# Neighbouring query blocks share one window of keys: band matmuls in pairs in a block-sparse attention with a gated feed-forward

## The chip, the cores and the metric

The kernel runs on one core of one Trainium2 chip. The metric is the device time of one execution in microseconds (us), as the median of several runs; lower is better.

## What is computed

Block-sparse attention over `q`, `k`, `v` of shape (4, 8, 768, 64), then a gated feed-forward on its result. Cut to what matters:

```python
block, n_blocks, window, scale = 32, 24, 1, 1/8
mask = |blk_i - blk_j| <= 1                       # band: own block and both neighbours
mask |= (blk_i == 0) | (blk_j == 0) | (blk_i == 23) | (blk_j == 23)   # blocks 0 and 23 are global
for qb in range(24):                               # three sampled key blocks for each query block
    for kb in sampled_blocks[qb]: mask[qb, kb] = True
attn = softmax(where(mask, scale * q @ k.T, -1e9)); y = attn @ v      # per batch and head
x = y as (4, 768, 512)
h = relu(x @ w_in)                                 # 512 -> 1024
c = conv of h along the sequence, width 3, one weight per tap and feature
out = (h * sigmoid(c)) @ w_out                     # 1024 -> 512, float32
```

The sampled blocks are data: they are read on the chip, and entries that the band, the global blocks or an earlier entry already cover are pointed at a block of zeros.

## The kernel before

The work is cut into eight half batches n (batch b = n // 2, half g = n % 2, 384 queries each). A half batch has four attention steps, one for each pair of heads hp, and then a feed-forward. There are thus 32 attention steps. Each has four parts:

- **s_a, the band scores** (line 862): one matmul for each of the 11 inner query blocks, 128 keys on the output partitions, 64 columns (32 queries of two heads). Even and odd blocks use windows that begin at different 32-key offsets (`win`). **e_a** (line 871) takes the exponential on ScalarE, with a bias of -30000 on partitions (from `bias_t`) that are not of the block.
- **s_g, the global scores** (lines 882 and 887): six matmuls of the keys against the one fully attending block of this half ("full", block 0 or 23), and four of the two global key blocks (KD) against all inner queries. **e_g** (line 894) is their exponential.
- **s_r, the sampled scores** (line 905): 11 matmuls against gathered keys KG. **e_r** (line 912) is their exponential.
- **a_fn, attention times values** (line 951): the probabilities are the stationary operand, 32 query columns of them, and 65 value columns (64 and a one for the sum) stream through. The output of query block j lands on 32 of 128 PSUM partitions, 32j to 32j+31. For each step there are 67 matmuls: per inner block and head one band and one sampled, per inner block one global over both heads, and 12 for the full block. They are issued round robin over the four j.

The values come by way of a DRAM copy: `v` is loaded, cast and widened by the ones (line 674, `vr`), written to DRAM (`vs`, line 684, rows of 520 elements in sequence order), and read back as VN in six chunks of 128 rows (line 693). VS is VN shifted by 64 rows, a copy between partitions (line 702). The sampled values VG are gathered from `vs` by DMAs whose offset is a register (line 801), three for each block, 33 for each half batch; the sampled keys KG are copied inside SBUF with register offsets (line 791) by VectorE and GpSimd. `WHO` says which queue issues which gather: SyncE (SP) or GpSimd (POOL). The offsets are unpacked from a packed table by integer division, remainder and multiplication on the issuing engine (`block_off`, with loads of the table in `reg_load`, line 748); a limited number is kept in registers.

The feed-forward: line 1117 multiplies by w_in, lines 1128 and 1130 apply relu, lines 1031 to 1058 are the convolution and the gate on VectorE with a tanh on ScalarE (line 1046), a part of the convolution goes to TensorE (line 1078), and line 1001 multiplies by w_out.

The order of the instructions on all engines is fixed when the program is built: every piece of work is an operation with a cost for each engine that may do it, a due time and buffers (`pl.op`), and `Plan.run` searches for an order by forward and backward passes with random changes. Its costs are constants written in the code: a_fn counts as 0.74 us on TensorE, a change of the kind of matmul (`mode` "F", "T" or "A" of an operation) as SWITCH = 0.09 us, and fetching a page of 256 TensorE instructions as FETCH = 2.3 us. The plan knows no change of kind inside one operation.

At the start, QB (queries, with zeros for the other head) and other buffers are set to zero by VectorE and GpSimd (lines 519 to 535).

Of the kernel before, what the change touches and what calls it, by code (L numbers as in the profile page):

```python
# [52 lines left out]
class Op:  # L53
    __slots__ = ("alts", "fn", "prio", "deps", "lat", "dma", "mode", "allocs", "uses", "earliest", "outs",
                 "pend", "ready", "start", "end", "eng", "key", "done", "seq", "after", "lazy", "n", "nd")
# [9 lines left out]
DMA_LAT = 1.9  # L65
SWITCH = 0.09
LAZY = 12.0
PAGE, FETCH = 256, 2.3
# [3 lines left out]
class Plan:  # L72
# [11 lines left out]
    def op(self, alts, fn, prio, deps=(), lat=None, dma=None, mode=None, alloc=(), uses=(), earliest=0.0,  # L84
           after=(), lazy=False, n=0, nd=1):
        o = Op(alts, fn, prio, [d for d in deps if d is not None], lat, dma, mode, earliest)
        o.key = len(self.ops)
        o.lazy = lazy
        o.n = n
        o.nd = nd  # L90
        o.after = [d for d in after if d is not None]
        for b in alloc:
            o.allocs.append(b)
            b.users.append(o)
        for b in uses:
            o.uses.append(b)
            b.users.append(o)
        self.ops.append(o)
        return o
# [14 lines left out]
    def forward(self, prio, first=True):  # L114
# [8 lines left out]
        count, pages = 0, {}  # L123
# [13 lines left out]
        while left:  # L137
            still = []
            for o in blocked:
# [12 lines left out]
                if ok:  # L152
                    rr = {}
                    for e in o.alts:
                        t = r
                        for d in o.deps:
                            t = max(t, self.avail(d, e))
                        rr[e] = t
# [142 lines left out]
    def run(self, passes=6, trials=40):  # L301
# [9 lines left out]
        for x in range(trials):  # L311
            prio = [p + shake.gauss(0.0, 1.0) for p in best[1]]
# [12 lines left out]
def kernel(  # L325
# [21 lines left out]
    ROW = H * 65  # L347
    WHOLE = ()
    PEC = (2,)
# [11 lines left out]
    vs_t = [dr.tile([S + 32, ROW], BF16, tag=f"vs{x}", name=f"vs{x}") for x in range(B)]  # L361
# [4 lines left out]
    KT = many(NKT, [128, 4, S + 32], BF16, "kt")  # L366
# [10 lines left out]
    pa_t = many(NPA, [128, 704], BF16, "pa")  # L377
    pr_t = many(NPR, [128, 704], BF16, "pr")
    pg_t = many(NPG, [128, 736], BF16, "pg")
# [97 lines left out]
    def biases(e):  # L477
        nc.vector.memset(bias_t, 0.0)
        nc.vector.memset(bias_t[0:32], -30000.0)
        nc.vector.memset(bias_t[96:128, 1:2], -30000.0)  # L480
# [8 lines left out]
    def blocks(e):  # L489
# [16 lines left out]
        v_.tensor_scalar(out=tm, in0=r, scalar1=-1.0, scalar2=float(NB), op0=ALU.mult, op1=ALU.add)  # L506
# [11 lines left out]
    for s in range(NKT):  # L518
        z_ops.append(op({"POOL": 0.2}, lambda e, s=s: nc.gpsimd.memset(KT[s][:, :, S:S + 32], 0.0), -6))
    qz = []  # L520
    for s in range(NQB):
        def zq(e, s=s):
            eng = nc.vector if e == "DVE" else nc.gpsimd
            eng.memset(QB[s][0:64, 1, :], 0.0)
            eng.memset(QB[s][64:128, 0, :], 0.0)
        qz.append(op({"DVE": 0.8} if s < 4 else {"POOL": 1.7}, zq, -6 + s))
    kz = []
    for s in range(NKD):
        kz.append(op({"POOL": 0.25}, lambda e, s=s: nc.gpsimd.memset(KD[s], 0.0), -6 + s))
    vz = []  # L530
    for s in range(NVN):
        vz.append(op({"POOL": 0.6}, lambda e, s=s: nc.gpsimd.memset(VD[s].rearrange("p a b -> p (a b)"), 0.0), 1 + s))
# [14 lines left out]
    for b in range(B):  # L547
        vs_zero.append(sp(lambda e, b=b: nc.sync.dma_start(out=vs_t[b][S:S + 32, :], in_=zrow), 4 + 8 * b, [z_row],
# [40 lines left out]
    def qk_pair(P):  # L589
# [52 lines left out]
        def kd(e):  # L642
            kt = KT[kt_buf[b].index][:, hp, 0:S].rearrange("q (n s) -> q n s", s=32)
            for h in range(2):
                r0 = 64 * h
                nc.gpsimd.tensor_copy(out=KD[kd_buf[P].index][r0:r0 + 64, r0:r0 + 64]
                                      .rearrange("q (n s) -> q n s", s=32), in_=kt[r0:r0 + 64, 0:NB:NB - 1, :])
        kd_w[P] = op({"POOL": 0.6}, kd, due - 1, [kev] + (kz[P:P + 1] if P < NKD else []), alloc=[kd_buf[P]], uses=[kt_buf[b]])
# [6 lines left out]
    def v_batch(b):  # L655
# [26 lines left out]
        for r in range(4):  # L682
            wr.append(op({"ACT": 0.9} if b == 0 and r % 2 else {"SP": 0.9}, lambda e, r=r: (
                nc.scalar if e == "ACT" else nc.sync).dma_start(
                out=vs_t[b][0:S].rearrange("(n c r) e -> n c r e", c=8, r=4)[:, :, r, :],
                in_=vr_t[rb_.index].rearrange("(n r) c h d -> n r c (h d)", r=4)[:, r]),
                -4 if b == 0 else due - 9, ros, dma=0.65, uses=[rb_]))
# [4 lines left out]
        for y in range(2):  # L692
            vn_w[b].append(sp(lambda e, y=y: nc.sync.dma_start(
                out=VN[vn_buf[b].index][:, 3 * y:3 * y + 3],
                in_=vs_t[b][384 * y:384 * y + 384].rearrange("(c p) e -> p c e", p=128)),
                due - 5, wr + [vm], 1.4, uses=[vn_buf[b]]))
        vs_w[b] = []
        for h in range(2):
            def sh(e, h=h):
                eng = nc.vector if e == "DVE" else nc.gpsimd  # L700
                r0, r1 = (64, 0) if h == 0 else (0, 64)
                eng.tensor_copy(out=VS[vn_buf[b].index][r1:r1 + 64], in_=VN[vn_buf[b].index][r0:r0 + 64, h:h + 5])  # L702
            vs_w[b].append(op({"DVE": 0.85} if b == 0 else {"POOL": 2.4}, sh, due - 3, vn_w[b], uses=[vn_buf[b]]))
        vd_w[b] = []
        for h in range(2):
            for x in range(2):
                def ldd(e, h=h, x=x):
                    eng = nc.vector if e == "DVE" else nc.gpsimd
                    src = VN[vn_buf[b].index][96 * x:96 * x + 32, 5 * x].rearrange("p (a h d) -> p a h d", h=2, d=65)
                    r0 = 64 * h + 32 * x  # L710
                    eng.tensor_copy(out=VD[vn_buf[b].index][r0:r0 + 32, :, 65 * h:65 * h + 65], in_=src[:, :, h, :])
                vd_w[b].append(op({"DVE": 0.25, "POOL": 0.45}, ldd, due - 3, vn_w[b][x:x + 1] + vz, uses=[vn_buf[b]]))
# [3 lines left out]
    raw, off = {}, {}  # L716
    why = "made on the chip from the checked table: block numbers from 0 to 24, in fields of five bits"
# [3 lines left out]
    def block_off(name, i, s, kg=False):  # L721
        kg = kg or name == "DVE"
# [3 lines left out]
        val = raw[(name, (i - 1) // 2)]  # L726
        val = (val // 2 ** (5 * f) if f else val)
        unit = 32 if kg else 32 * ROW
        val = (val % 32 if f < 5 else val) * unit
        val = nc.s_assert_within(val, 0, NB * unit, skip_runtime_bounds_check_because=why)  # L730
        if len([1 for k_ in off if k_[0] == name]) < 48:
            eng = HW[name]
            r = eng.alloc_register(name=f"off{name}{i}_{s}{kg}")
            eng.reg_alu(r, eng.compute_val(val), 0, ALU.add)
            val = off[(name, i, s, kg)] = eng.snap(r, min_val=0, max_val=NB * unit)
        return val

    loads = {}

    def reg_load(name, blocks_, prio, after=(), early=()):  # L740

        ys = sorted({(i - 1) // 2 for i in blocks_} - {y for n_, y in raw_seen if n_ == name})
        for y in ys:
            raw_seen.add((name, y))

        def fn(e):
            for y in ys:
# [4 lines left out]
            for i in early:  # L752
                for s in range(3):
                    block_off(name, i, s)
        return op({name: 0.5 * len(ys) + 0.7 * len(early)}, fn, prio, [blk] + [o for (n_, i), o in loads.items() if n_ == name],
                  after=after)
    raw_seen = set()
    KPX = 3
    WHO = [["SP"] * 7 + ["POOL"] * 4] + [["SP"] * 11] + [["SP"] * 8 + ["POOL"] * 3, ["SP"] * 11] * (B - 1)

    def gd_dur(n, x, en):
        if en != "SP":
            return 1.7
        return 1.15 if n == 0 or n > 1 and (n % 2 or x < 7) else 1.8

    def gathers(n):
# [7 lines left out]
        need = {"DVE": set(range(NX - KPX)), "POOL": set(range(NX - KPX, NX))}  # L774
        for x in range(NX):
            need.setdefault(WHO[n][x], set()).add(x)
        for en, xs in need.items():
            new = [i0 + x for x in sorted(xs) if (en, i0 + x) not in loads]
            if new:
                o = reg_load(en, new, -7 if n == 0 else 6, [o for o in vg_w[0] if en in o.alts] if n else [],  # L780
                             [i0 + x for x in range(NX) if WHO[n][x] == en] if n == 0 else [])
                for i in new:
                    loads[(en, i)] = o
        for x in range(NX):
            en = "POOL" if x >= NX - KPX else "DVE"

            def cp(e, x=x):
                eng = nc.vector if e == "DVE" else nc.gpsimd
                for s in range(3):
# [3 lines left out]
            kg_w[n].append(op({en: (0.70 if n < 2 else 0.40) if en == "DVE" else 0.85}, cp, due - 3 + 0.2 * x,  # L793
                              [loads[(en, i0 + x)], km] + kt_w[b] + kgz, uses=[kg_buf[n], kt_buf[b]]))
        vg_w[n] = []
        for x in range(NX):
            en = WHO[n][x]

            def gd(e, x=x):
                for s in range(3):  # L800
                    HW[e].dma_start(out=VG[vg_buf[n].index][32 * s:32 * s + 32, x, :],  # L801
                                    in_=vs_t[b].rearrange("r e -> (r e)")[bass.ds(block_off(e, i0 + x, s), 32 * ROW)].rearrange(
                                        "(r e) -> r e", e=ROW))
            vg_w[n].append(op({en: gd_dur(n, x, en)}, gd, due - 3 + 0.5 * x, [loads[(en, i0 + x)], vm]
                              + vs_rows[b], dma=0.33, nd=3, uses=[vg_buf[n]]))
# [3 lines left out]
    for P, x in ((0, 0), (0, 1), (1, 0), (2, 0), (3, 0), (1, 1), (2, 1), (3, 1)):  # L809
# [17 lines left out]
    for b in range(1, B):  # L827
        v_batch(b)
        for P in range(4 * b, 4 * b + 4):
# [8 lines left out]
    def attention(n, hp):  # L838
# [5 lines left out]
        band = sorted(inner, key=lambda i: (i != 1 and i % 2, i))  # L844
# [8 lines left out]
        def win(i):  # L853
            return 32 * (i - 1) if i % 2 else 32 * (i - 2)

# [3 lines left out]
        def s_a(e):  # L859
            st = st_t[sa.index]  # L860
            for w, i in enumerate(band):
                nc.tensor.matmul(out=st[:, 64 * w:64 * w + 64].rearrange("p (h s) -> p h s", h=2),  # L862
                                 lhsT=kt()[:, win(i):win(i) + 128], rhs=qcol(i), start=True, stop=True)
        so = op({"PE": 11 * 0.029}, s_a, due - 0.6, qb_w[P] + kt_w[b], mode="F", alloc=[sa],
                uses=[kt_buf[b], qb_buf[P]], after=[prev_s], n=22)
        prev_s = so

        def e_a(e):
            cuts = [(0, 384, 0), (384, 704, 2)] if g == 0 else [(0, 320, 0), (320, 384, 1), (384, 704, 2)]
            for c0, c1, z in cuts:  # L870
                nc.scalar.activation(out=pa_t[pa.index][:, c0:c1], in_=st_t[sa.index][:, c0:c1], func=AF.Exp,  # L871
                                     bias=bias_t[:, z:z + 1] if z < 2 else 0.0, scale=0.125)
# [334 lines left out]
```

## Time and profile before

| | us |
|---|---|
| median of 3 runs (lowest, highest) | 263.32 (262.34, 268.49) |
| the profiled execution | 267.39 |
| its span, first to last instruction | 265.6 |
| TensorE matmul busy | 210.4 (79%), 4266 instructions |
| TensorE weight load busy | 145.6 (55%), 4281 instructions |
| VectorE busy | 192.3 (72%) |
| ScalarE busy | 162.9 (61%) |
| GpSimd busy | 109.7 (41%) |
| mean granted TensorE clock | 0.916 of full |

How to read it: busy time of TensorE is the union of its matmuls' modelled durations, and matmuls overlap, so a duration of 0.2 us is mostly latency; the distance between the starts of consecutive matmuls tells what one occupies. In the list of groups, "128\*32 128x65" is the stationary operand (rows\*columns) and the moving one. In a timeline, consecutive instructions of one group are merged into a row with a count. "Issue" is time in which an engine waited for nothing that the profile shows.

### The profile page before, as it was taken

To read this page: it belongs to the slowest core of one execution; us is meant where nothing else is said; L and a number is where in the kernel's file an instruction comes from. 1 tells how busy PE (TensorE), PEld (TensorE's weight loads), DVE (VectorE), ACT (ScalarE), POOL (GpSimd) and SP (SyncE) were. 2 spreads that over 40 slices of the span, in tenths; PEclk is the share of its full clock that TensorE was granted. 3 is DMA by queue.
4 is the path that set the end of the run, shared out by engine and by line. 5 is a ranking of instruction groups with operands and counts; after the bars stand their busy time and mean duration, and the time that the engine had idled before them with its cause. 6 is when DMAs were issued, how large, how long until landed. Compare 5 with 4: busy or idle time off the path is not lost.

```text
span 265.6 us, 11219 instructions
## 1 busy us (share of the span) xinstructions
PE 210.4 (79%) x4266; PEld 145.6 (55%) x4281; DVE 192.3 (72%) x651; ACT 162.9 (61%) x296; POOL 109.7 (41%) x225
## 2 busy tenths in 40 slices
PE   5393836998849958859857897994999999899984
PEld 1272635865546614657536666663675666776531
DVE  7555752399839999637969986814699996479992
ACT  2185705698527931728925695672697889677651
POOL 8476992440609992220899340056248000000000
PEclk9999957699998977979985998899899999999999
DMA  6995998796795834677782475366552341300033
GB/s 71 205 223 163 174 215 170 125 179 117 116 213 155 188 87 91 141 169 164 189 177 59 126 126 128 79 156 182 166 84 61 64 125 47 121 6 2 0 118 118
DMA packets 34218, 33.87 MB, mean 128 GB/s; under 512 B 5709, under 2 KB 30470, under 8 KB 34166
## 3 DMA queue, kind: packets, MB, share of 16 engines
q0 software_dynamic: 13216, 12.84, 31.0%
q1 hardware_dynamic: 20542, 19.93, 26.7%
q8 instruction: 33, 0.54, 0.8%
q10 hardware_dynamic: 408, 0.40, 0.5%
q14 instruction: 19, 0.16, 0.2%
HBM read 35.06 MB, written 9.62 MB: 168 GB/s over the span
## 4 chain that ended last, share of the span: by engine, by line
PE 42%; DVE 23%; issue 11%; DMA 10%; SPq 7%; ACT 4%; POOL 1%; DVEq 1%; POOLq 0%; ACTq 0%
PE mix L1117 12%; PE mix L951 9%; PE mix L1001 6%; SPq L801 6%; DVE m L1031 5%; DVE gT L1058 4%; PE mix L610 3%; DMA vg<-vs 3%; DVE kg L791 3%; DMA hE<-in_q_dram 3%; PE st L905 3%; DVE m L1038 3%; PE st L862 2%; PE st L887 2%; DMA vs<-vr 2%
## 5 line engine op out<-in xcount | busy, mean ns | idle before, releaser
L1001 PE MATMUL mix<-woutb,gT 128*128 128x512 bf16 x177 | 48.4, 396 | 8.7 <-DVE gT L1058 5.9
L1117 PE MATMUL mix<-xT,winb 128*128 128x384 bf16 x256 | 49.2, 339 | 2.9 <-DVE o2s L1011 2.3
L791 DVE COPY kg<-kt 128x128 bf16 x192 | 36.3, 248 | 7.6 <-issue 4.3
L1031 DVE TENSOR_SCALAR m<-hE,cw 128x384 bf16<-128x384 bf16 x144 | 37.6, 331 | 2.2 <-ACT hE L1128 2.0
L951 PE MATMUL mix<-vg,pr 96*32 96x65 bf16 x704 | 30.6, 205 | 9.6 <-DMA vg<-vs 6.0
L1128 ACT ACTIVATE hE<-mix 128x384 bf16<-128x384 f32 x52 | 25.4, 494 | 17.2 <-PE mix L1117 15.6
L1117 PEld LDWEIGHTS <-winb 128*128 128x128 bf16 x256 | 24.8, 101 | 18.8 <-issue 5.6
L912 ACT ACTIVATE pr<-st 128x704 bf16<-128x704 f32 x32 | 24.3, 761 | 13.2 <-PE st L905 13.2
L801 POOL DMA_DIRECT2D vg<-vs x39 | 20.2, 520 | 29.4 <-DMA vg<-vs 19.0
L951 PE MATMUL mix<-vs,pa 128*32 128x65 bf16 (+1 forms) x320 | 29.4, 206 | 2.4 <-DVE vs L702 2.4
L1001 PEld LDWEIGHTS <-gT 128*128 128x128 bf16 x192 | 17.0, 101 | 26.3 <-DVE gT L1058 9.0
L871 ACT ACTIVATE pa<-st,bias 128x384 bf16<-128x384 f32 (+2 forms) x48 | 21.1, 474 | 14.8 <-PE mix L951 12.1
L951 PEld LDWEIGHTS <-pr 96*32 96x32 bf16 x704 | 24.3, 102 | 10.2 <-DMA vg<-vs 6.2
L951 PEld LDWEIGHTS <-pg 128*32 128x32 bf16 x736 | 23.8, 103 | 10.8 <-issue 10.6
L951 PE MATMUL mix<-vd,pg 128*32 128x130 bf16 x352 | 26.8, 238 | 1.9 <-issue 1.9
L1046 ACT ACTIVATE m<-m 128x768 bf16<-128x768 bf16 x24 | 20.3, 861 | 11.7 <-DVE m L1038 11.7
L894 ACT ACTIVATE pg<-st 128x736 bf16<-128x736 f32 x32 | 25.5, 797 | 2.8 <-PE st L887 2.7
L791 POOL COPY kg<-kt 128x128 bf16 x72 | 22.4, 353 | 10.9 <-ACT kt L621 10.4
L1038 DVE TENSOR_TENSOR m<-m 128x768 bf16<-128x768 bf16 x48 | 25.9, 561 | 0.1
L951 PE MATMUL mix<-vn,pa 96*32 96x65 bf16 (+1 forms) x384 | 26.0, 206 | 0.0
L951 PEld LDWEIGHTS <-pa 128*32 128x32 bf16 (+1 forms) x704 | 22.7, 100 | 2.4 <-issue 2.1
L951 PE MATMUL mix<-vn,pg 128*32 128x65 bf16 x384 | 21.0, 205 | 3.2 <-issue 3.2
(106 smaller groups left out, 427.0 us busy)
## 6 DMA issues: line engine op xcount, KB each, us to landing
vg<-vs SPq DMA_DIRECT2D x225, 32.5 KB
out_dram<-o2s SPq DMA_DIRECT2D x24, 256.0 KB
vn<-vs SPq DMA_DIRECT2D x8, 390.0 KB
vs<-vr SPq DMA_DIRECT2D x14, 195.0 KB
vst<-in_v_dram POOLq DMA_DIRECT2D x7, 384.0 KB, 7.9
nat<-in_k_dram POOLq DMA_DIRECT2D x12, 192.0 KB, 4.4
nat<-in_q_dram POOLq DMA_DIRECT2D x12, 192.0 KB, 5.4
vg<-vs POOLq DMA_DIRECT2D x39, 32.5 KB, 3.3
```

Source lines behind the costliest of these rows:

```text
L791: eng.tensor_copy(out=dst[:, :, x, 32 * s:32 * s + 32], in_=KT[kt_buf[b].index][:, :, bass.ds(block_off(e, i0 + x, s, True), 32)])
L801: HW[e].dma_start(out=VG[vg_buf[n].index][32 * s:32 * s + 32, x, :], in_=vs_t[b].rearrange("r e -> (r e)")[bass.ds(block_off(e, i0 + x, s) ...
L871: nc.scalar.activation(out=pa_t[pa.index][:, c0:c1], in_=st_t[sa.index][:, c0:c1], func=AF.Exp, bias=bias_t[:, z:z + 1] if z < 2 else 0.0, ...
L894: nc.scalar.activation(out=pg_t[pg.index], in_=st_t[sg.index][:, 0:736], func=AF.Exp, bias=0.0, scale=0.125)
L912: nc.scalar.activation(out=pr_t[pr.index], in_=st_t[sr.index][:, 0:704], func=AF.Exp, bias=0.0, scale=0.125)
L951: nc.tensor.matmul(out=dst, lhsT=l_, rhs=r_, start=(y == 0), stop=(y == len(lists[j]) - 1), skip_group_check=True)
L1001: nc.tensor.matmul(out=mix_t[mb.index], lhsT=gT_t[gt_buf[n].index][:, ffc, 128 * c:128 * c + 128], rhs=woutb[:, ffc, :], start=(ffc == 0), ...
L1031: nc.vector.tensor_scalar(out=mv(dst)[:, y], in0=hE_t[heb.index][:, f0 + y, c0 + tp_:c0 + tp_ + cn], scalar1=cw[:, tp_, f0 + y:f0 + y + 1] ...
L1038: nc.vector.tensor_tensor(out=m[:, 0], in0=m[:, 0], in1=m[:, x], op=ALU.add)
L1046: th = op({"ACT": t_act(W)}, lambda e: nc.scalar.activation(out=m_t[cb.index][:, 1], in_=m_t[cb.index][:, 0], func=AF.Tanh, bias=0.0, scal ...
L1117: nc.tensor.matmul(out=mix_t[hb.index][:, 0:384], lhsT=winb[:, fc, 128 * ffc:128 * ffc + 128], rhs=xT_t[xt_buf[n].index][:, fc, :], start= ...
L1128: nc.scalar.activation(out=dst, in_=src, func=AF.Relu, bias=0.0, scale=0.5)
```

## The change

- **Band in pairs.** Query blocks 2p and 2p+1 share one window of 128 keys, 64p-32 to 64p+95. s_a becomes 6 matmuls of 128 columns in place of 11 of 64. e_a becomes two exponentials over 32-column stretches, one for the even and one for the odd blocks, each with its own bias column.
- **a_fn.** The global matmuls come first, one for each third t of the half with all 128 query columns stationary (3 in place of 11). Then for each t and head: the band matmuls with 64 query columns of a pair stationary (32 where one block of the pair is the full block, with 64 key rows), the full block's six where it lies in this third, and three or four sampled ones with 32 query columns. That is 49 matmuls in place of 67. The plan counts the step as 0.68 us.
- **Values 32 rows off.** VN holds rows 32 to 799, so that the pair windows are aligned with its chunks; one more small write (`head`) repeats the first 32 rows behind the last. Rows in `vs` are 1024 elements apart. The full block's keys are taken 32 later too, without blocks 0 and 23, which the global matmuls add.
- **Offsets** are unpacked by one mask and one shift for each, in operations of their own (`offsets`) that the plan can place, up to 16 blocks for each engine kept in registers; for the first half batch they are ordered behind the writes of `vs` on the same queue. SP gets 7, 7, 8, 9, 8, 9, 8, 9 of the 11 gathers of the halves and GpSimd the rest (before: 7, 11, 8, 11, 8, 11, 8, 11).
- **Zeros.** QB, KD and VD are zeroed by copies on ScalarE.
- **Plan.** Other constants (DMA latency 2.4, FETCH 4.2, a first page offset of 63), a `slack` for some operations, 150 random trials in place of 40; KD copies may go to VectorE.

```diff
-DMA_LAT = 1.9
+DMA_LAT = 2.4
-PAGE, FETCH = 256, 2.3
+PAGE, FETCH, FIRST = 256, 4.2, 63
...
+    NSP = (7, 7, 8, 9, 8, 9, 8, 9)
...
-            eng.memset(QB[s][0:64, 1, :], 0.0)
-            eng.memset(QB[s][64:128, 0, :], 0.0)
-        qz.append(op({"DVE": 0.8} if s < 4 else {"POOL": 1.7}, zq, -6 + s))
+            zero = warm[:, 0:384].unsqueeze(1).broadcast_to([128, 2, 384])
+            for h in range(2):
+                nc.scalar.copy(out=QB[s][64 * h:64 * h + 64, 1 - h, :].rearrange("p (a b) -> p a b", a=2),
+                               in_=zero[64 * h:64 * h + 64])
+        qz.append(op({"ACT": 1.42}, zq, -6 + s, [w0]))
...
+        head = sp(lambda e: nc.sync.dma_start(
+            out=vs_t[b][S:S + 32, 0:ROW].rearrange("(c r) e -> r c e", c=8),
...
-                in_=vs_t[b][384 * y:384 * y + 384].rearrange("(c p) e -> p c e", p=128)),
-                due - 5, wr + [vm], 1.4, uses=[vn_buf[b]]))
+                in_=vs_t[b][384 * y + 32:384 * y + 416, 0:ROW].rearrange("(c p) e -> p c e", p=128)),
+                due - 5, wr + [vm] + [head] * y, 1.45, uses=[vn_buf[b]], slack=1.0 if b else 0.0))
...
-        val = raw[(name, (i - 1) // 2)]
-        val = (val // 2 ** (5 * f) if f else val)
-        unit = 32 if kg else 32 * ROW
-        val = (val % 32 if f < 5 else val) * unit
...
+        at = 5 if kg else 15
+        eng.reg_alu(r, eng.compute_val(raw[(name, (i - 1) // 2)]), 31 << (5 * f), ALU.bitwise_and)
+        if 5 * f < at:
+            eng.reg_alu(r, r, at - 5 * f, ALU.logical_shift_left)
+        elif 5 * f > at:
+            eng.reg_alu(r, r, 5 * f - at, ALU.logical_shift_right)
...
+        def behind(en):
+            if n == 0:
+                return [o for o in vs_rows[0][:4] if en in o.alts]
...
-            for w, i in enumerate(band):
-                nc.tensor.matmul(out=st[:, 64 * w:64 * w + 64].rearrange("p (h s) -> p h s", h=2),
-                                 lhsT=kt()[:, win(i):win(i) + 128], rhs=qcol(i), start=True, stop=True)
+            if g == 0:
+                nc.tensor.matmul(out=st[:, 0:128].rearrange("p (h o s) -> p h o s", h=2, o=2)[:, :, 0],
+                                 lhsT=kt()[:, 32:160], rhs=qcol(1), start=True, stop=True)
+            for p in range(1 - g, 6):
+                o = 64 * (6 * g + p)
+                nc.tensor.matmul(out=st[:, 128 * p:128 * p + 128].rearrange("p (h s) -> p h s", h=2),
+                                 lhsT=kt()[:, o - 32:o + 96], rhs=QB[qb_buf[P].index][:, :, o:o + 64],
+                                 start=True, stop=True)
...
-            lists = [[] for _ in range(4)]
...
+            mm = []
+            for t in range(3):
+                mm.append((o_[:, t, :], pg_t[pg.index][:, 384 + 128 * t:512 + 128 * t], vd[:, hp, :], t == 0, False))
+            for t in range(3):
+                i0 = 12 * g + 4 * t
+                for h in range(2):
+                    hc = 65 * (2 * hp + h)
+                    for j in (0, 2):
+                        p = (i0 + j) // 2
+                        vt, vc = (vn, p // 2) if p % 2 or p == 0 else (vs, p // 2 - 1)
+                        k1, j0, w = 128, j, 64
+                        if i0 + j == full:
+                            k1, j0, w = 64, j + 1, 32
+                        elif i0 + j + 1 == full:
+                            k1, w = 64, 32
+                        c0 = 128 * (p - 6 * g) + 64 * h
+                        mm.append((o_[32 * j0:32 * j0 + w, t, 65 * h:65 * h + 65], pa_t[pa.index][0:k1, c0:c0 + w],
+                                   vt[0:k1, vc, hc:hc + 65], False, False))
+                    if 0 <= full - i0 < 4:
+                        j = full - i0
+                        for c in range(6):
+                            k1 = 128 if c < 5 else 64
...
+                    for j in range(4):
+                        if i0 + j != full:
...
+            for dst, l_, r_, first_, last_ in mm:
+                nc.tensor.matmul(out=dst, lhsT=l_, rhs=r_, start=first_, stop=last_, skip_group_check=True)
+        ao = op({"PE": 0.68}, a_fn, due + 2.6, [ea, eg, er] + vn_w[b] + vs_w[b] + vd_w[b] + vg_w[n], mode="A",
+                alloc=[ab], uses=[pa, pg, pr, vn_buf[b], vg_buf[n]], after=[prev_av], n=98)
```

## The prediction, made before the changed kernel was run

> **What bounds the kernel now.** I read the page first, then the busy time by stretch, the chain of waits, the waits by engine, and last the timeline of TensorE around single steps.
>
> The busy time by stretch shows where TensorE has room:
>
> ```profile
> core 0: us, PE busy (x) PEld busy (x) DVE busy (x) ACT busy (x) POOL busy (x), PEclk, DMA share, GB/s
> 16.00:40.00 24.00, 13.62 (x282) 10.97 (x282) 14.66 (x62) 12.57 (x21) 21.21 (x48) 0.89 0.91 189
> 40.00:190.00 150.00, 120.67 (x2599) 85.53 (x2596) 105.90 (x331) 90.82 (x169) 70.82 (x125) 0.87 0.67 144
> 190.00:250.00 60.00, 57.07 (x1261) 39.80 (x1265) 51.57 (x188) 49.15 (x94) 8.18 (x26) 1.00 0.25 62
> ```
>
> From 190 to 250 us TensorE is idle for 2.9 of 60 us: what is added there lengthens the run. From 40 to 190 it is idle for 29.3 of 150 us, at a mean clock of 0.87. The page's chain agrees that TensorE leads:
>
> ```profile
> PE 42%; DVE 23%; issue 11%; DMA 10%; SPq 7%; ACT 4%; POOL 1%; DVEq 1%; POOLq 0%; ACTq 0%
> PE mix L1117 12%; PE mix L951 9%; PE mix L1001 6%; SPq L801 6%; DVE m L1031 5%; DVE gT L1058 4%; PE mix L610 3%; DMA vg<-vs 3%; DVE kg L791 3%; DMA hE<-in_q_dram 3%; PE st L905 3%; DVE m L1038 3%; PE st L862 2%; PE st L887 2%; DMA vs<-vr 2%
> ```
>
> Line 951, the step that the change rewrites, holds 8.6% of it by the full chain, 22.8 us of its 36.0 us of busy time. "Issue" holds 10.5%; its pieces inside or beside runs of line 951 (2.51, 3.58, 3.19, 1.94 us) are TensorE waiting for nothing visible, and the waits put most of that idle time there:
>
> ```profile
> PEld L951 <- issue: 16.3, 22, 3.3
> PE mix L951 <- issue: 8.7, 5, 3.2
> ```
>
> What decides this case is how matmuls of different tile shapes follow one another. Two answers of the timeline, at full clock:
>
> ```profile
> 198.59 0.38 PE L951 MATMUL mix<-vn,pg 128*32 128x65 bf16 x7
> 198.90 0.49 PE L610 MATMUL mix<-ident,nat 96*64 96x96 bf16 x14
> ```
>
> ```profile
> 124.30 0.48 PE L862 MATMUL st<-qb,kt 128*128 128x64 bf16 x11
> 124.62 0.81 PE L1117 MATMUL mix<-xT,winb 128*128 128x384 bf16 x4
> ```
>
> In the first the shape goes from 32 to 64 stationary columns. The last of line 951 ends at 198.97 and lasts 0.19, so it starts at 198.78; the next line starts at 198.90, 0.12 later, where 65 columns stream in 0.027: 0.095 is lost. In the second the shape stays 128\*128 across lines: 11 matmuls start within 0.32, 29 ns each (64 columns at 2.4 GHz are 27), and nothing is lost. Over all neighbouring matmuls of the trace, start to start less columns at 2.4 GHz, no change of shape class costs under 95 ns (128 to 32: 96; 128 to 64: 96; 32 to 64: 97; 32 to 128: 98; 64 to 128: 98), and staying in a class between two lines costs 2 to 3 ns where nothing is awaited. Before the change every matmul of line 951 has 32 stationary columns, so a step pays only on entry and exit.
>
> [...]
>
> **The change part by part**, against the profiled span of 265.6 us (execution 267.39, 4.1 above the median of 263.32; I carry the difference over to the median unchanged).
>
> *a_fn.* Now: 67 matmuls that start within 0.64 to 0.79 us where no stall falls (0.76 from 198.02 to 198.78), plus entry and exit at 0.1 each, so 0.92. After: three global ones with 128 columns, then for each of six (third, head) pairs a band part with 64 columns and a sampled part with 32, so 1 + 11 changes; in the third with the full block, the band piece cut to 64 rows, and the full block's last chunk with 64 rows, add three more for each head. 18 changes. Step length: 2 x 57 for the first globals, 54 + 96 into the band, 17 x (27 + 96), two runs of four gaps at 30 for the full block (the spacing of the x7 row), and 20 gaps of 9 ns between parallel neighbours (195.79 to 195.83 has four): 114 + 150 + 2,091 + 240 + 180 = 2.78 us. One change out: 0.12. Together 2.90, so +1.98 for each step; I take 1.95. From the other side, if a change inside the step were free the 18 x 96 ns go and it is 2.78 - 1.73 = 1.05, or 0.68 as the plan counts: -0.2 to +0.2. If only the column shape counts and not the 64 rows, 13 changes: +1.5. I take the upper value, since every kind of change that the trace shows costs the same.
>
> On the path: stretch 190 to 250 holds 670 records of line 951, ten steps: 19.5 us, all of it. About two steps lie before 40 us: 3.9 us, all of it, TensorE being what the first outputs wait for. The other 20 add 39 us; the chain runs through about half of line 951's busy time there, and 29 us of idle time can take up the rest: 19.5. Sum +43.
>
> *Fewer instructions.* s_a goes from 22 to 12 and a_fn from 134 to 98, so 46 x 32 = 1,472 fewer of 8,547, 27.6 blocks for 33.4[...]. Of the 11.2 us of issue pieces on the chain I take 9 away: -9. The plan's new FETCH figures serve the same.
>
> *Scores.* s_a: 11 x 29 = 0.32 us becomes 6 x 56 = 0.34; s_g gains 64 columns, 27 ns. 32 x 0.04 = +1.3.
>
> *ScalarE.* e_a now takes 36.9 us of busy time over 32 steps (14.1, 9.4, 8.4 and 5.0 in its four forms), 1.15 a step; two of about 0.58 are 1.16. e_g: 797 ns x 768/736, +0.03. Hidden behind TensorE: +0.3. Zeros: QB five times two copies of about 0.79 (as the 64x768 copies of line 636), KD five at 0.25, VD two at 0.55, 10 us. ScalarE is idle from 2.4 to 11.7 us, which covers 9; the last ones move into a stretch where it is half idle. 0; without that cover, +4 ahead of the first key copies. In return VectorE loses eight memsets of 0.38 and GpSimd 3.6 us.
>
> *Start.* The second `vr` copy ends at 10.5 us, but SP writes `vs` only at 14.09, since its loads and divisions come first:
>
> ```profile
> 14.09 1.85 SPq L684 DMA_DIRECT2D vs<-vr  x2
> 15.98 1.45 SPq L551 DMA_DIRECT2D gT<-in_moe_conv_w_dram  x1
> 20.87 0.43 SPq L693 DMA_DIRECT2D vn<-vs  x1
> ```
>
> Now the writes come first, up to 3.5 us earlier, less 0.45 for `head`, and the unpacking (7 blocks at 0.5 by the plan) runs while they travel, ahead of the gathers. The gathers queued behind, and the first a_fn at 37.87 us, follow: -3. If the DMA rings (share 0.9 to 1.1 there) hold them back, 0. If unpacking lasts beyond the writes' landing, the gathers slip by what is left over, under 1.
>
> *Queues.* SP issues 65 blocks of gathers for 75, at 1.45 to 1.8 us; three `head` writes follow at 0.45. GpSimd gets 30 more issues at 0.52, 15.6 us, queued ahead of KD, KG and VS copies which s_g, s_r and a_fn await; its idle 59% covers it. Net -1.5; if not covered, see the rivals. Pitch 1024: rows of 1,040 bytes as before, 0.
>
> Sum: 43 - 9 + 1.3 + 0.3 - 3 - 1.5 = +31. 263.3 + 31 = 294.
>
> **Rivals.**
> 1. *Changes of shape inside a step are free or overlap* (faster). For it: 64 to 32 columns with no line between is never seen before, and the plan counts 0.68. Against: all five kinds seen cost 95 or more. Then a_fn gives about 0, and the rest stands: 263.3 - 9 + 1.3 + 0.3 - 3 - 1.5 = 251, 250 with the plan's value. It decides as soon as a step grows by less than 0.55 us (12 us of gains over the 22 steps' worth on the path), about 30 ns for each of 18 changes.
> 2. *The drains fall into idle time.* For it: 29 us idle from 40 to 190. Against: 190 to 250 has none, and gives 19.5 alone. With 13 cheap changes and nothing outside: 263.3 + 15 - 12 = 266, no clear change.
> 3. *GpSimd is late.* For it: in 131.8 to 148.7 it works without a pause. Its extra 5 us per odd half would then stand before KG copies three times: with free changes, 251 + 15 = 266; added to the main case, 309.
> 4. *The clock falls.* [...] the clock was 0.67 between 40 and 50 us around a stalled step. With the step's streaming part doubled, +1 us x 22: 316.
>
> **How the numbers follow.** Main case 0.76, own range 276 to 318; rival 4 and the worse half of 3 0.06; rival 2 and the milder half of 3 0.06, mostly no change; rival 1 0.12. Slower by over 2% 0.82, within 2% 0.06, faster 0.12; 2% is about what a measurement of this kernel can tell from no change. The likeliest is 294. Range 268 to 322: below it are rival 1 and most of 2, above it part of 4, 0.2 in all. Its width comes from 13 or 18 changes (12 us), the share on the path (about 10 either way) and the clock.
>
> **What would show it.** Right: starts within an undisturbed a_fn spread over 2.3 to 2.9 us, with about 120 ns at each turn from 64 to 32 columns; TensorE near full from 40 us on; issue waits at line 951 well under 16 us; `vs` writes from SP near 11 us. Wrong: a_fn within 0.7 to 1.05 us (rival 1), or GpSimd releasing s_r through KG (rival 3).

## The result, and the profile after

The changed kernel takes 339.82 us (336.97 to 344.7, 4 runs) against 265.05 us (262.34 to 268.49, 4 runs) before: 1.289 times, 95% interval 1.272 to 1.306. Some executions are over 1.5% longer than the fastest of their kernel; the times given are medians of all executions, while the ratios to before, with their 95% intervals, leave those out. The profiled execution took 341.71 us with a span of 340.0 us, 74.4 more than before. Here are the busy times, the granted clock and the chain of waits on its page:

```profile
PE 299.5 (88%) x3529; PEld 201.1 (59%) x3545; DVE 189.5 (56%) x655; ACT 174.8 (51%) x294; POOL 121.0 (36%) x237
...
PEclk9558557967996965779785959769679769878799
...
PE 70%; DVE 12%; DMA 9%; SPq 3%; issue 3%; ACT 1%; POOL 0%; DVEq 0%; ACTq 0%; POOLq 0%
PE mix L961 32%; PE mix L1126 11%; PE mix L1010 9%; PE st L912 3%; DMA vs<-vr 3%; DVE m L1040 3%; PE st L868 3%; SPq L805 3%; PE st L894 3%; PE st L1087 3%; PE mix L983 3%; DMA vn<-vs 3%; DMA hE<-in_v_dram 2%; PE mix L618 2%; DVE gT L1067 2%
```

TensorE issues 17% fewer matmuls and is busy for 89 us longer. Line 961 is the values step (951 before). By the full chain it holds 31.9% of 340.0, 108.4 us, where it held 22.8: +86 on the chain. Its busy time went from 36.0 to 113.1 us, +77. Everything else on the chain shrank by 11, issue from 28 to 10 us among it. VectorE's wait for the step, before and after (us in total, times, longest):

```profile
DVE rcp L962 <- PE mix L951: 21.3, 16, 3.8
...
DVE rcp L971 <- PE mix L961: 77.4, 29, 4.5
```

One step at full clock, from the timeline of TensorE (start, duration, what):

```profile
65.79 0.33 PE L961 MATMUL mix<-vd,pg 128*128 128x130 bf16 x3
66.05 0.22 PE L961 MATMUL mix<-vs,pa 128*64 128x65 bf16 x1
66.05 0.22 PE L961 MATMUL mix<-vn,pa 128*64 128x65 bf16 x1
66.20 0.21 PE L961 MATMUL mix<-vg,pr 96*32 96x65 bf16 x4
66.34 0.22 PE L961 MATMUL mix<-vs,pa 128*64 128x65 bf16 x1
66.35 0.22 PE L961 MATMUL mix<-vn,pa 128*64 128x65 bf16 x1
66.50 0.21 PE L961 MATMUL mix<-vg,pr 96*32 96x65 bf16 x4
...
67.38 0.20 PE L961 MATMUL mix<-vn,pa 64*32 64x65 bf16 x1
67.51 0.46 PE L961 MATMUL mix<-vn,pg 128*32 128x65 bf16 x6
```

A turn from 64 to 32 columns and back shows as starts 0.14 to 0.15 us apart, where 65 columns stream in 0.027 us. (Matmuls of 384 and of 512 columns in one shape start 163 and 216 ns apart at full clock, before and after, so 128 columns more take 53 ns, 2.4 columns per ns; that is the rate that the prediction takes off.) Two matmuls of 64 columns start together, within 3 to 4 ns, and so do four of 32: inside a shape no such loss shows. The 64-row piece at 67.38 loses time both before and after it. Over the parts at full clock the median loss is 121 ns from 64 to 32 columns, 107 back, 96 from 32 columns into 64 rows and 104 out of them. Where the prediction and the expectations say drain, they mean this time between starts; what TensorE does in it the traces do not show.

Three steps in a row, in the busy time by stretch (length; busy time and count of each engine; clock, DMA share, GB/s):

```profile
264.40:267.30 2.90, 2.90 (x50) 2.06 (x48) 1.59 (x13) 2.40 (x4) 0.00 (x0) 1.00 0.41 153
267.40:271.10 3.70, 3.70 (x49) 2.44 (x45) 1.69 (x4) 0.98 (x2) 0.00 (x0) 0.56 0.06 21
271.30:275.20 3.90, 3.90 (x53) 2.54 (x49) 0.75 (x2) 0.00 (x0) 0.00 (x0) 0.50 0.00 0
```

The same 49 matmuls take 2.92, 3.69 and 3.91 us from first to last start as the clock goes from 1.00 to 0.56 and 0.50. This is the usual picture, with exceptions: the 32 steps lie in 16 runs of one to three; 13 of the 16 first steps have clock 1.00, but one of the 11 second ones and none of the five third ones. The column of TensorE's busy time says nothing of it, since it is full in all three.

At the start, SyncE's part of the timeline after:

```profile
9.60 1.85 SPq L692 DMA_DIRECT2D vs<-vr  x2
11.49 0.56 SPq L559 DMA_DIRECT2D gT<-in_moe_conv_w_dram  x1
15.20 0.32 SPq L696 DMA_DIRECT2D vs<-vr  x1
21.17 1.87 SPq L805 DMA_DIRECT2D vg<-vs  x3
```

The writes of the values copy go out at 9.60 in place of 14.09 us, and the first gather starts at 21.17 in place of 21.51: the chain has a transfer of 10.35 us there where it had 5.71.

### The profile page after: what moved, and what is told of

Its sections match the earlier page's. It is cut to its first block, busy times and chain, and to the rows that moved or that the text cites. A ratio compares the mean times of both kernels' runs of the same rounds, so it can differ in the third digit from the quotient of the medians.

```text
span 340.0 us, 9985 instructions
## 1 busy us (share of the span) xinstructions
PE 299.5 (88%) x3529; PEld 201.1 (59%) x3545; DVE 189.5 (56%) x655; ACT 174.8 (51%) x294; POOL 121.0 (36%) x237
## 4 chain that ended last, share of the span: by engine, by line
PE 70%; DVE 12%; DMA 9%; SPq 3%; issue 3%; ACT 1%; POOL 0%; DVEq 0%; ACTq 0%; POOLq 0%
PE mix L961 32%; PE mix L1126 11%; PE mix L1010 9%; PE st L912 3%; DMA vs<-vr 3%; DVE m L1040 3%; PE st L868 3%; SPq L805 3%; PE st L894 3%; PE st L1087 3%; PE mix L983 3%; DMA vn<-vs 3%; DMA hE<-in_v_dram 2%; PE mix L618 2%; DVE gT L1067 2%
## 5 line engine op out<-in xcount | busy, mean ns | idle before, releaser
L971 DVE RECIPROCAL rcp<-mix 128x6 f32<-128x6 f32 x32 | 6.3, 195 | 77.6 <-PE mix L961 77.4
L961 PE MATMUL mix<-vn,pa 128*64 128x65 bf16 (+1 forms) x224 | 49.4, 230 | 0.0
L805 POOL DMA_DIRECT2D vg<-vs x69 | 37.6, 548 | 31.4 <-PE mix L961 23.0
L961 PE MATMUL mix<-vg,pr 96*32 96x65 bf16 x704 | 43.9, 218 | 4.2 <-DMA vg<-vs 4.2
L878 ACT ACTIVATE pa<-st,bias 128x384 bf16<-128x384 f32 x64 | 32.8, 565 | 26.5 <-PE mix L961 18.7
L961 PE MATMUL mix<-vs,pa 128*64 128x65 bf16 x160 | 37.8, 237 | 0.0
L961 PEld LDWEIGHTS <-pa 128*64 128x64 bf16 (+1 forms) x384 | 28.4, 111 | 15.7 <-issue 1.4
L961 PEld LDWEIGHTS <-pg 128*32 128x32 bf16 (+2 forms) x480 | 29.0, 106 | 10.9 <-issue 0.5
L961 PE MATMUL mix<-vn,pg 128*32 128x65 bf16 (+1 forms) x384 | 34.4, 219 | 0.0
L589 POOL DMA_DIRECT2D nat<-in_k_dram x12 | 7.7, 643 | 65.9 <-PE mix L618 62.6
L901 ACT ACTIVATE pg<-st 128x768 bf16<-128x768 f32 x32 | 26.0, 812 | 9.3 <-PE st L894 7.6
```

Source lines behind the costliest of these rows:

```text
L878: nc.scalar.activation(out=pa_t[pa.index].rearrange("p (k o s) -> p k o s", o=2, s=32)[:, k0:, x], in_=st_t[sa.index][:, 0:768].rearrange( ...
L901: nc.scalar.activation(out=pg_t[pg.index], in_=st_t[sg.index][:, 0:768], func=AF.Exp, bias=0.0, scale=0.125)
L961: nc.tensor.matmul(out=dst, lhsT=l_, rhs=r_, start=first_, stop=last_, skip_group_check=True)
```

## The experiments

My theory S: each change of shape inside a step costs the 0.1 us measured above, and the clock falls in steps that lose so much time. Rival Q: the gather split, the zeros or the new plan cost the time. In e1 to e4 the kernel before, run beside them, took 268.45 us.

**Only the order of the 49 matmuls.** The same matmuls, grouped by shape (`turns` deals them out in turn over the four output blocks):

```diff
...
+            mm = [m for m in mm if m[1].shape[1] > 64] + [m for m in mm if m[1].shape[1] == 64] + turns(
+                [m for m in mm if kind(m) == (True, 32)]) + turns([m for m in mm if kind(m) == (False, 32)])
             for dst, l_, r_, first_, last_, _, _ in mm:
```

> The changed kernel with the 49 matmuls of each a_fn only reordered: three with 128 columns, then all with 64, then those with 32 in turn over the four output blocks, the 64-row ones last, so 3 changes of shape inside a step in place of 18. Theory S[...]: a step takes 1.1 to 1.3 us, the clock comes back to about 0.9, and the time falls to 252 to 266. Rival Q (the gather split between the queues, the later zeros or the new plan cost the time): it stays above 310, since those are untouched.

Measured: 266.71 us, 1.007 of before (0.996 to 1.018). The undisturbed steps, those with no wait inside, take 1.14 to 1.18 us. The beginning of one, in which five pairs of 64 columns follow at 0.03 to 0.05 us in place of 0.29:

```profile
46.47 0.33 PE L969 MATMUL mix<-vd,pg 128*128 128x130 bf16 x3
46.73 0.22 PE L969 MATMUL mix<-vn,pa 128*64 128x65 bf16 x1
46.74 0.22 PE L969 MATMUL mix<-vs,pa 128*64 128x65 bf16 x1
46.78 0.20 PE L969 MATMUL mix<-vn,pa 128*64 128x65 bf16 x1
```

Its chain of waits:

```profile
PE 52%; DVE 19%; DMA 14%; issue 6%; ACT 3%; SPq 3%; DVEq 0%; POOL 0%; ACTq 0%; POOLq 0%
PE mix L969 14%; PE mix L1018 12%; PE mix L1134 10%; DMA vg<-vs 6%; DVE m L1048 6%; DMA vs<-vr 4%; PE st L912 4%; DVE m L1055 3%; PE st L894 3%; DMA hE<-in_v_dram 3%; PE st L868 2%; DVE kg L794 2%; SPq L805 2%; DVE gT L1075 2%; PE mix L991 2%
```

The values step (L969) falls from 32% of 340 to 14% of 267.5 us. Reordering alone takes back the whole 73 us: S stands and Q falls. No other difference is left: this kernel and the one by thirds below leave the plan's costs alone, and their traces show the same order of work as the changed kernel, on all four engines and in the DMA queues. The time is 0.7 above my band. On the chain the values step still holds 37.6 us, 15 more than before, and everything else 13 less: what the other parts gain may be spent on a step that is still 0.4 us longer than before. This run can't tell the two apart.

**The values step of before on the new layout.** Stationary operands of 32 columns for all 68 matmuls, in turn over the four blocks:

```diff
...
+            mm = [(*l[y], y == 0, False) for y in range(max(len(l) for l in ls)) for l in ls if y < len(l)] + [
+                (*m, False, True) for m in late]
...
-        ao = op({"PE": 0.68}, a_fn
+        ao = op({"PE": 0.85}, a_fn
```

> The changed kernel with the values step of before on the new layout: 68 matmuls with 32 stationary columns, in turn over the four output blocks, the four 64-row ones last (1 change inside a step), counted as 0.85 us by the plan. Everything else of the change stays. Theory S: a step takes about 0.8 us, and what is left of the change shows alone: 250 to 258 by my sum of the other parts. Rival Q: above 300.

Measured: 272.55 us, 1.018 of before (1.003 to 1.034), and a step of 0.88 to 0.90 us, 1.00 to 1.03 to the start of the next line. A miss: I had the rest of the change at 12 us of gain, and here it shows none. The expectation was wrong in itself: 9 of the 12 us were for fewer TensorE instructions, and this kernel does not have them (148 a step for scores of the band and values together, where before has 156 and the change 110). So the waits for issue are as before:

```profile
PEld L960 <- issue: 15.3, 22, 3.7
...
PE mix L960 <- issue: 8.7, 5, 3.5
```

The step's own growth, about 0.15 us over the 0.86 to 0.88 of before, explains some 5 us of loss.

**Seven changes in place of 18.** Grouped by thirds:

```diff
...
+            mm = [m for m in mm if m[1].shape[1] > 64] + [
+                m for t in range(3) for m in [m for m in mm if m[6] == t and m[1].shape[1] == 64] + turns(
+                    [m for m in mm if m[6] == t and kind(m) == (True, 32)])] + turns(
+                [m for m in mm if kind(m) == (False, 32)])
```

> The changed kernel with a_fn ordered by thirds: 7 changes of shape inside a step. Theory S, with 0.11 us for each change as the trace after shows between 64 and 32 columns: 11 x 0.11 less than 2.92 us, so 1.7 us a step at full clock, and a time of 268 to 290, between the other two. If only the clock matters and not the count of changes, it lies near the changed kernel (over 320) or near the grouped one (under 262).

Measured: 278.45 us, a step of 1.61 to 1.63 us, clock 0.919. From 3 to 7 changes the run grows by 11.7 us, 92 ns for each of 4 x 32; from 7 to 18 by 61.4, 174 ns for each of 11 x 32. At full clock a step grows by 115 and 118 ns for each change in the two parts (1.16, 1.62, 2.92 us). So the first slope is the loss at the changes, some of it off the path, and the second is more: at 118 ns the 11 x 32 changes account for at most 42 of the 61 us. The other 20 or so fit the clock, which has gone from 0.919 to 0.783.

**The plan told the truth.** One constant:

```diff
-        ao = op({"PE": 0.68}, a_fn
+        ao = op({"PE": 2.9}, a_fn
```

> The changed kernel with one constant of the plan changed: a_fn counts as 2.9 us in place of 0.68. The 18 changes stay. Theory S (TensorE is full of drains): 320 to 342, the lower end if the plan sets other matmuls between the steps and the clock stays up. Rival P (the order planned for 0.68 us wastes the time): below 300.

Measured: 340.0 us (338.5 to 341.5), clock 0.820 in the profiled run. Rival P, that the order planned for 0.68 us wastes the time, falls as far as this constant tests it: the plan drew another order and took the same time.

**The clock by itself.** Theory C: the clock falls because the changes take some two thirds of a step. The 18 changes stay, and more columns stream between them, into PSUM columns that nothing reads. The kernel before took 268.81 us beside this and the next three. (`k` is the stationary shape of a run of matmuls `ms`.)

```diff
...
+                if k[0] == 96 or k[1] == 64:
+                    mm += [(spare[32 * m[5]:32 * m[5] + k[1]], m[1], m[2], False, True, m[5], m[6])
+                           for y in range(3) for m in ms]
```

> The changed kernel with more streaming between its 18 changes of shape: each group of sampled matmuls and of 64-column band matmuls is issued three more times into PSUM columns that nothing reads, about 12 groups x 3 x 27 ns = 0.97 us more in each step, 3.9 us at full clock. Theory C[...]: the second and third of consecutive steps are no slower than the first, the mean clock rises above 0.88, and the time is only about 350. Without C (the added work simply adds, at the clock of the changed kernel): second and third steps of 4.7 us and more, 370 to 385.

Measured: 363.23 us (361.46 to 364.99). The stretches of two pairs of consecutive steps:

```profile
202.40:206.60 4.20, 4.20 (x147) 3.22 (x145) 4.20 (x5) 0.49 (x1) 3.47 (x2) 1.00 0.24 59
206.70:210.80 4.10, 4.10 (x153) 3.20 (x145) 2.73 (x12) 2.53 (x5) 0.00 (x0) 1.00 0.22 47
268.00:272.10 4.10, 4.10 (x146) 3.18 (x144) 0.69 (x1) 0.72 (x2) 0.00 (x0) 1.00 0.02 4
272.20:276.40 4.20, 4.20 (x154) 3.27 (x145) 0.75 (x2) 1.26 (x3) 2.98 (x6) 1.00 0.35 79
```

The second of each pair keeps clock 1.00, as in five of the six pairs of this run (one has 0.67; of the single steps one ran at 0.50, and the very first at 0.55); the mean clock is 0.900 for 0.783. A step of 145 matmuls takes 4.05 to 4.08 us, hardly more than the unfilled one at half clock (3.91). The kernel by thirds agrees, in the very order of the changed one: nine of its 11 second steps have clock 1.00. By my estimate from the losses above, columns stream for about half of a step in these two kernels and for a third in the changed one. So with the 18 changes kept, and more matmuls between them, the clock is 1.00 in most second steps, where one of 11 has it in the changed kernel. Whether streamed columns or started matmuls count is not shown, since both grew together. The time lies between my two values: the fill cost 1.15 us a step at full clock where I had 0.97, 37 us in all, of which 23 show. The other 13 or so are about what the clock was worth, though this kernel's order was drawn anew.

**The plan's constants on the kernel before.** Only these lines, and the count's start at FIRST:

```diff
-DMA_LAT = 1.9
+DMA_LAT = 2.4
-PAGE, FETCH = 256, 2.3
+PAGE, FETCH, FIRST = 256, 4.2, 63
...
-    def run(self, passes=6, trials=40):
+    def run(self, passes=6, trials=150):
...
-            prio = [p + shake.gauss(0.0, 1.0) for p in best[1]]
+            prio = [p + shake.gauss(0.0, 2.0) for p in best[1]]
```

> The kernel before with the five new constants of the plan only (latency 2.4, fetch 4.2, first page offset 63, 150 trials, wider random changes). The step of my forecast that gave 9 us to fetch stalls put them down to fewer instructions, with the plan serving the same: if the plan's figures do it, 256 to 261 here and fewer issue waits at the values step than 16 us; if they do nothing by themselves, 264 to 270.

Measured: 270.99 us, 1.011 of before (1.003 to 1.018), 1 us above the higher of my two ranges. The issue waits at its values step fall to 8.1 us, but over all weight loads they stay (35.4 us for 35.8): the stalls move to other lines. The constants give nothing by themselves.

**The grouped order, with its cost told to the plan** (1.17 for 0.68):

> The grouped kernel (3 changes of shape inside a step) with the plan told its measured 1.17 us in place of 0.68. If the order matters once TensorE is not full of drains: 258 to 264. If not, within 1% of the grouped one's 266.7.

Measured: 266.05 us, 0.993 of before (0.987 to 1.000): within 1% of the untold one.

**The band at 32 columns as well**, 59 matmuls, 2 changes:

```diff
...
-                        mm.append((o_[32 * j0:32 * j0 + w, t, 65 * h:65 * h + 65], pa_t[pa.index][0:k1, c0:c0 + w],
+                        for y in range(w // 32):
+                            mm.append((o_[32 * (j0 + y):32 * (j0 + y) + 32, t, 65 * h:65 * h + 65],
...
```

> The grouped kernel with the band part of a_fn at 32 columns too, so three matmuls of 128 columns and 56 of 32 with 2 changes of shape inside a step, counted as 0.9 us. By the spacing of before (about 27 to 30 ns for each turn of four) and 0.1 us a change: 1.0 us a step against 1.15, so 5 us less on a full TensorE, but 20 more instructions a step: 260 to 267.

Measured: 268.64 us, 1.001 of before (0.992 to 1.011), 1.6 us above my range, with a step of 0.97 to 1.00. The shorter step came, the time did not: issue holds 14% of its chain, against 6 and 9% in the two grouped kernels with 20 fewer instructions a step.

**Parts of the change.** In these three the kernel before took 267.51 us. First, on the kernel before, the offsets behind the first writes:

```diff
-                o = reg_load(en, new, -7 if n == 0 else 6, [o for o in vg_w[0] if en in o.alts] if n else [],
+                o = reg_load(en, new, -7 if n == 0 else 6, [o for o in vg_w[0] if en in o.alts] if n else [o for o in vs_rows[0][:4] if en in o.alts],
```

> The kernel before with one part of the change: for the first half batch SP and GpSimd load and unpack the offsets only behind the writes of the values copy on the same queue. My forecast took 3 us for it; the trace after shows the writes issued 4.5 us earlier and landing at the same time. If the start is bound by issue: 0.985 to 0.99 of before, first gathers before 19 us. If by the transfers on the rings: no change beyond 1%, first gathers at 21 us again.

Measured: 274.05 us, 1.025 of before (1.007 to 1.044), which lies outside both of my values. Its writes start at 10.85 us and its first gathers at 23.05. An earlier write buys no earlier gather here. Why the rest became slower I can't say; the order is drawn anew whenever an operation or a dependence changes.

Second and third, on the grouped and told kernel, the gather split of before (`NSP = (7, 11, 8, 11, 8, 11, 8, 11)`), and the memsets of before:

> The grouped and told kernel (266.05 us) with the gathers split as before: SP 7, 11, 8, 11 and so on of 11, GpSimd the rest. If the split is worth the 1.5 us that I took, 1.003 to 1.01 of it; if GpSimd's extra issues cost more than SP saves, faster than it; either way it is far from the 75 us of the change.

> The grouped and told kernel (266.05 us) with QB, KD and VD zeroed by VectorE and GpSimd as before. I took this part at nothing, covered by ScalarE's idle start: within 1% of 266. If it cost the start, the first values step begins over 2 us earlier here.

Measured: 259.77 us for the split, 0.981 of before (0.966 to 0.995), and 263.18 us for the zeros, with runs from 257.68 to 267.67, 0.976 of before (0.958 to 0.995). Which of the two is faster is not shown. With the zeros of before, the first values step begins at 33.43 us for 32.59, so the zeros on ScalarE did not delay it. All issue waits of weight loads in the split version sum to 16.4 us, where the told kernel has 27.8 and before has 35.8. Both together (before took 267.37 us beside it):

> The grouped and told kernel with both the gathers split and the buffers zeroed as before, so what is left of the change is the band in pairs, the values 32 off, the offsets and the plan. If split and zeros each cost something by themselves, it is faster than the 259.8 us of the old split alone: 254 to 259. If the spread of the last kernels is the redrawn order and the fetch stalls that fall with it, it may land anywhere from 258 to 267.

Measured: 273.21 us, 1.018 of before (1.008 to 1.027), outside the range. So these two parts don't add. Four kernels that differ only in split and zeros lie at 259.8 to 273.2 us, and I can't tell a part's own worth from that of the order that was drawn with it. It was not tried to hold one order fixed over them.

## Why the prediction was wrong

The direction was right, and so was a loss at every change of shape; the size was 31 where 75 came, and all that is missing lies in the values step.

- *Cost of a change of shape*: I carried 96 ns over from pairs that the trace before had to one it had not. Measured 96 to 121; neighbours of one shape start 3 to 4 ns apart, for my 9. The step at full clock is 2.92 us from first to last start and 3.05 to the next step's, for my 2.78 and 2.90: about 5 us over 32 steps. Rival 1 was wrong, and the reading of 13 changes too, as the 64-row pieces show.
- *On the path* is the step that failed first. I let half of the 20 middle steps' growth sink into 29 us of idle time and counted 22 steps' worth, 43 us. The chain after holds 108.4 of the step's 113.1 us: 32 steps' worth, 62. That idle time was not free room: when a step trebles, what waited for other work before waits for TensorE. VectorE's wait for this step alone rose from 21.3 to 77.4 us. The share of the step that lies on the path was no constant to carry over: it grew with the step, from 63% before to 78% (e1), 83% (e3) and 96%.
- *The clock* is the second. I had it as rival 4 with 0.06, apart from the main case, where it was a part of it. Start to start, steps take 3.05, 3.86 and 4.07 us in a row; the mean busy time of 3.53 is about 0.5 over the first, 16 us in all by estimate. In e5 and e3, with more between the changes, the mean clock is 0.900 and 0.919, for 0.783 in the changed kernel.
- *Fetch stalls*: in the changed kernel the chain's issue fell by 17.5 us, for the 9 that I took. Why more fell is not shown. The other runs point to a gain of about the size of my term: in the five grouped kernels with 49 matmuls a step (e1, e7, e10, e11, e12) the chain's issue is 15 to 25 us in the profiled execution, and in those with 59 to 68 (before, e2, e6, e8, e9) 28 to 37. Their orders differ, and e8 with 59 has the most, so its size is not shown. That these are fetches of instructions fits the traces. The DMA queue of the kind "instruction" (q8) moves 33 packets of 16 KB before, one for 259 TensorE records, 28 after, one for 253, and 52 in e5, one for 254; so my 27.6 blocks for 33.4 came out. In the trace before, a packet of it, 0.89 to 1.07 us long, is under way in each of the six issue stalls of weight loads above 2 us (the other 27 packets meet none). Counted over the TensorE records, weight loads included, four of the six come at numbers 961, 2239, 3261 and 5051, nearly the same place in a block of 256 each time.
- *Start*, -3: wrong; my stated other side (0) is what happened, here and in e9, though that the rings did it is not shown apart from the longer transfer (10.35 us for 5.71). The first values step, too, gained nothing: it began at 32.55 us and waited until 37.87 for its sampled values, which I read as its start, and after the change it waits until 38.50. *Scores, ScalarE*: nothing in the chain after speaks against them. ScalarE did the zeros by 13.9 us, the last three ahead of its second key copy. *Queues*, -1.5: not shown.

The sum with what was measured: 62 + 5 + 16 for the step is 83, 3 short of its 86 on the chain, and 86 less the 11 that everything else gave back is 75. My other terms had come to 12 less. That they agree as a sum is in part luck, since the start gave nothing and issue gave twice its term.

## What to carry to other kernels

Count the changes of stationary shape in an instruction list, not only its matmuls: fewer and wider matmuls lost here because widths alternate (18 changes a step, at 96 to 121 ns each), and sorting them by width took the loss back with nothing else changed. When an addition makes the leading engine full, put all of it on the path, and ask what the same addition does to the clock. A plan that is drawn at random again with each edit moves the time by some per cent, so a part's worth below that is read from several draws, or from an edit that leaves the drawn order alone, or left open.

## What was not expected of the hardware

TensorE had matmuls in flight all the time, busy for 3.90 of 3.90 us in the third step shown above, and its granted clock was 0.50 there. In the changed kernel, whose shape changes take about two thirds of a step by my estimate (18 at 0.11 of 2.92 us), the clock mostly fell in second and third steps, to 0.50 to 0.53 in all five third ones; in the row shown above the third begins 6.9 us after the first. With more matmuls between the same changes (e5) it was 1.00 in the second step of five of six pairs.
